# A gated long convolution beside a feed-forward layer on one core: a new opening, and a new written order for everything after it

## The chip, the cores and the metric

The kernel runs on one core of one Trainium2 chip. The metric is the device time of one execution in microseconds (us): 199.13 us before the change, the median of three runs that lie between 199.11 and 199.16 us. The core has five engines with a queue of instructions each: TensorE (PE in the profile: matrix multiplies and transposes, written to eight PSUM banks), VectorE (DVE), ScalarE (ACT: activations and copies), GpSimd (POOL, here mostly an issuer of DMAs) and SyncE (SP, which issues the other DMAs). An engine takes its instructions in the order in which they were written and stops at the first one whose inputs or buffers are not ready.

## The reference

All tensors are bf16 and the batch is 1: 2048 positions of 640 channels, and a hidden layer of 1728.

```python
x  = A_q
xn = layernorm(x)                                   # over the 640 channels
# branch A: short convolution, gate, long convolution by FFT, skip, gate
k_shift = sum_t k_pad[:, t:t+S] * shift_k[:, 3-t]   # 4 taps
kv = k_shift * A_v
y  = irfft(rfft(kv, 2S) * rfft(A_ssm_k, 2S))[:S] + kv * A_ssm_D
s  = xn * y
# branch B: feed-forward on the same normalised rows
g  = silu(gelu(xn @ w1 + b1) @ w2 + b2)
out = x + s * g
```

## The kernel before

**Tiling.** Position n of the sequence is row n // 16 of the 128 partitions and column n % 16. Sixteen consecutive columns make four chunks of four (`xn_tiles[c]`), and branch B goes chunk by chunk: `x_tr` (steps `tt`) transposes a normalised chunk into `xnT`, `ffn1` (`h`, 14 per chunk, five matmuls of 128x512 each; the last of a chunk has ten small ones) and its gelu on ACT (`he`) fill `hT`, `ffn2` (`g`, eight per chunk, 14 matmuls of 128x320 each) multiplies by w2, ACT takes the silu (`ge`), and DVE multiplies it into the normalised rows (`gm`).

**The long convolution** is a Fourier transform of 8192 points in two stages, written as matmuls with sine tables. The filter goes first: transposes (`kt`, cast out of PSUM by `kc`), first stage with the tables WA and WB (`kf`, out by `ke`), a store to DRAM that regroups the rows (`ks`), a load (`fl`), second stage (`ff`, out by `fe`), and a copy with swapped rows made by DMA (`mk`). The signal `kv` is built on DVE in 64 whole-row products and sums (`cv`), goes through the first stage (`uf`, out by `ue`), a store to DRAM (`us`) and a load (`ml`), and the second stage (`mu`). DVE multiplies it with the filter straight from PSUM, twice per tile (`mp`, `mq`: 96 products), PE transforms back (`ma`, `mb`, out by `me`), and after a last trip through DRAM (`ms` store, `yl` load) `y` does the last stage, `yt` multiplies with the rows of branch B and the result goes out (`yo`, `ys`; in the last chunk `ga`, `gs`).

**Small matmuls.** `ff`, `mu`, `ma` and `mb` work on 32 rows at a time. `blocks` (line 410) issues four matmuls of 32x32 weights for each of them; the table `TURNS` gives, for each of the 48 tiles of a stage, by how many places the output part is turned against the input part, so which four of the sixteen 32x32 parts of the array the four matmuls use.

**What sets the order.** No scheduler moves anything. `prologue()` writes the opening by hand: the constants, chunk 0's normalisation, transposes and the first six tiles of `ffn1`. Then a loop over the words of `PLAN` writes 1190 steps, one call each. A word is a step and its number, with `.a` or `.d` where either ACT or DVE can do it (casts out of PSUM, some normalisations). PSUM banks (`one`) and the SBUF slots of `area` (`pair`, `flat`) are handed out while this list is read, in its order, so a new order also changes which buffer a step takes and whom it has to wait for. `use_table` loads ACT's function tables where the order changes between gelu and the silu and sine set.

**The opening's end** (lines 823 to 843) goes: five tiles of `first_block(0, i)` on the first two columns, with a transpose of the packed small parameters `prm` behind the fourth; DVE's copy of the bias `b1_f` out of that transpose; the normalisation of columns 2 and 3; the copy `dD_sb`; the angles of the small 32x32 matrices (`small_bits`, `small_first`, `small_second`); the transposes `turn(2)`, `turn(3)`; the sixth `first_block`; `turned_out`, which copies those transposes to `xnT`, three fifths on DVE and two on ACT; and the six tiles of `first_block(1, i)` that read them.

## Time and profile before

| | us |
|---|---|
| median of 3 runs | 199.13 |
| the profiled execution | 199.48 |
| its span, first to last instruction | 197.7 |
| PE busy | 188.0 |
| DVE busy | 175.1 |
| ACT busy | 162.4 |
| POOL busy | 43.0 |

How to read it: busy time is the union of an engine's instructions; matmuls are pipelined and their ends are modelled, so two engines that are both near their span in busy time may differ a great deal in what they could still take. A row of the profile gives the line of the kernel, the engine, the operation, the tile written and read with its shape, a count, and the busy time with the mean duration of one. In the trace's rows by time, the second number is from the first start to the last end of a run of equal instructions. Consecutive instructions overlap at their ends, so that the distance between starts is shorter than a duration. A wait is put down to the instruction whose signal came last.

### The profile page before, as it was taken

Reading aid. Unit: us, or ns where it says so; the run is one execution under the profiler, and the core shown is the slowest. Engines: PE = TensorE matmul, PEld = TensorE weight load, DVE = VectorE, ACT = ScalarE, POOL = GpSimd, SP = SyncE. Lnnn points to the kernel's source line nnn. Section 1 sums busy time; section 2 is a strip of 40 time slices with the busy share of each in tenths; the row PEclk is TensorE's granted clock in tenths of the full one; section 3 lists DMA queues with packets and bytes.
Section 4 is the critical chain, followed back from the end, with each engine's and each line's share of the span. In section 5 each row is a group of like instructions: output and inputs, shape, how many; then the busy total and the mean of one; then the engine's idle time right before and its main releaser. Section 6 shows DMA issues by size and latency. Waiting matters only on the chain.

```text
span 197.7 us, 5098 instructions
## 1 busy us (share of the span) xinstructions
PE 188.0 (95%) x1913; PEld 110.7 (56%) x1925; DVE 175.1 (89%) x377; ACT 162.4 (82%) x322; POOL 43.0 (22%) x76
## 2 busy tenths in 40 slices
PE   7989989899999999998999999999999999999991
PEld 2566447786665455663565444365665544657770
DVE  7889998999999999989999999999999920489992
ACT  3458899999999999999998999999779758991030
POOL 8100200003455032255022000000466410002220
PEclk9999999999999999999999999999999999999999
DMA  6999999962878999798689899596869659994343
GB/s 202 375 385 348 355 411 412 395 243 103 328 302 339 297 318 368 275 360 323 252 277 332 260 356 317 196 297 239 254 243 339 237 169 327 395 396 184 148 175 138
DMA packets 27057, 57.69 MB, mean 292 GB/s; under 512 B 3032, under 2 KB 15513, under 8 KB 27032
## 3 DMA queue, kind: packets, MB, share of 16 engines
q1 hardware_dynamic: 22528, 39.65, 57.2%
q0 software_dynamic: 4320, 17.70, 24.1%
q8 instruction: 15, 0.25, 0.5%
q14 instruction: 10, 0.08, 0.2%
q10 hardware_dynamic: 184, 0.01, 0.1%
HBM read 33.76 MB, written 18.35 MB: 264 GB/s over the span
## 4 chain that ended last, share of the span: by engine, by line
PE 72%; ACT 17%; DVE 6%; issue 3%; POOL 0%; POOLq 0%; ACTq 0%; DVEq 0%
PE banks L493 23%; PE banks L467 21%; ACT area L147 8%; PE banks L414 7%; PE banks L533 5%; ACT hT L479 4%; PE banks L769 3%; PE banks L751 3%; PE banks L522 2%; PE banks L702 2%; ACT sl L499 2%; PE banks L451 2%; PE banks L703 2%; DVE area L573 2%; PE banks L463 1%
## 5 line engine op out<-in xcount | busy, mean ns | idle before, releaser
L147 ACT CAST area<-banks 128x426 bf16<-128x426 f32 (+2 forms) x175 | 80.7, 628 | 3.9 <-PE banks L414 3.4
L493 PE MATMUL banks<-w_sb,hT 128*128 128x320 bf16 x448 | 65.7, 299 | 0.5 <-ACT sl L499 0.4
L493 PEld LDWEIGHTS <-hT 128*128 128x128 bf16 x448 | 42.8, 98 | 19.5 <-issue 4.1
L467 PE MATMUL banks<-xnT,w_sb 128*128 128x512 bf16 x218 | 52.8, 379 | 0.7
L657 DVE TENSOR_TENSOR area<-banks,area 128x426 bf16<-128x426 f32 (+1 forms) x96 | 50.2, 594 | 0.2
L479 ACT ACTIVATE hT<-banks,b_f 128x512 bf16<-128x512 f32 x52 | 35.4, 719 | 5.6 <-PE banks L467 3.0
L467 PEld LDWEIGHTS <-w_sb 128*128 128x128 bf16 x230 | 21.5, 97 | 25.8 <-issue 3.7
L499 ACT ACTIVATE sl<-banks 128x320 bf16<-128x320 f32 x32 | 14.8, 489 | 14.5 <-PE banks L493 13.2
L577 DVE TENSOR_TENSOR area<-area 128x1280 bf16<-128x1280 bf16 x32 | 25.4, 818 | 0.3
L414 PE MATMUL banks<-area,mats 32*32 32x426 bf16 (+1 forms) x768 | 20.7, 345 | 0.5 <-DVE area L148 0.2
L711 DVE TENSOR_TENSOR area<-banks,xn 128x426 bf16<-128x426 f32 (+1 forms) x18 | 10.0, 595 | 12.3 <-ACT hT L479 10.2
L687 POOL DMA_DIRECT2D scrC<-area x16 | 11.7, 732 | 42.1 <-ACT area L147 40.0
L573 DVE TENSOR_TENSOR area<-area 128x1280 bf16<-128x1280 bf16 x24 | 19.1, 814 | 0.0
L533 PE MATMUL banks<-area,WA 128*128 128x212 bf16 (+1 forms) x64 | 15.6, 299 | 0.1
L548 POOL DMA_DIRECT2D scrK<-area x16 | 8.8, 554 | 30.2 <-DVE area L577 23.5
L533 PE MATMUL banks<-area,WB 128*128 128x214 bf16 (+1 forms) x64 | 15.3, 299 | 0.0
L414 PEld LDWEIGHTS <-mats 32*32 32x32 bf16 x768 | 8.1, 88 | 12.4 <-issue 10.1
L148 DVE CAST area<-banks 128x426 bf16<-128x426 f32 (+1 forms) x21 | 11.4, 594 | 1.7 <-PE banks L414 0.8
L559 POOL DMA_DIRECT2D scrU<-area x16 | 8.7, 546 | 14.7 <-ACT area L147 13.8
L430 POOL TENSOR_TENSOR rs<-ve,mhalf 128x4 f32<-128x4 f32 x3 | 4.1, 1351 | 31.1 <-DVE ve L426 31.1
L421 DVE BATCH_NORM_STATS2 st<-xn 128x6 f32<-128x320 bf16 x24 | 10.4, 473 | 0.0
L505 DVE TENSOR_TENSOR xn<-xn,sl 128x320 bf16<-128x320 bf16 x32 | 9.7, 314 | 0.7 <-ACT sl L499 0.7
(106 smaller groups left out, 198.3 us busy)
## 6 DMA issues: line engine op xcount, KB each, us to landing
scrK<-area POOLq DMA_DIRECT2D x16, 320.0 KB, 3.0
scrU<-area POOLq DMA_DIRECT2D x16, 320.0 KB, 4.1
area<-scrK SPq DMA_DIRECT2D x16, 320.0 KB, 6.5
area<-area SPq DMA_DIRECT2D x32, 160.0 KB, 4.2
area<-scrU SPq DMA_DIRECT2D x16, 320.0 KB, 4.2
scrC<-area POOLq DMA_DIRECT2D x16, 320.0 KB, 4.2
area<-scrC SPq DMA_DIRECT2D x16, 320.0 KB, 6.6
area<-in_A_k_dram SPq DMA_DIRECT2D x4, 640.0 KB, 10.0
```

The lines of the kernel that those rows point to most:

```text
L147: return nc.scalar.copy(out=out_ap, in_=in_ap)
L148: return nc.vector.tensor_copy(out=out_ap, in_=in_ap)
L414: nc.tensor.matmul(out=out[b, :], lhsT=mats[a, m, a], rhs=rhs[a, :], start=start, stop=stop)
L467: nc.tensor.matmul(out=ps, lhsT=w1_sb[:, t, ft * P:(ft + 1) * P], rhs=xnT[:, t, :], start=(t == 0), stop=(t == DT - 1))
L479: nc.scalar.activation(out=hT[:, ft, :], in_=one(("h", i)), func=ACT.Gelu_apprx_tanh, bias=b1_f[:, ft:ft + 1], scale=1.0)
L493: nc.tensor.matmul(out=ps[:, 0:HALF], lhsT=hT[0:M, ft, q * P:(q + 1) * P], rhs=w2_sb[0:M, ft, hs], start=(ft == 0), stop=(ft == FT - 1))
L499: nc.scalar.activation(out=sl[:], in_=one(("g", i))[:, 0:HALF], func=ACT.Silu)
L533: nc.tensor.matmul(out=ps[:, dst], lhsT=(WA, WB)[r][:, n2, :], rhs=rows[:, n2 % 2, src], start=True, stop=True)
L573: nc.vector.tensor_tensor(out=uc, in0=uc, in1=tmp, op=ALU.add)
L577: nc.vector.tensor_tensor(out=tmp if s else uc, in0=kh[:, r0:r0 + KC, :], in1=w_exp[:, j:j + 1, :].to_broadcast([P, KC, D]), op=ALU.mult)
L657: nc.vector.tensor_tensor(out=flat(("p", i))[:, x * w:x * w + w], in0=one(("mu", i))[:, 0:w], in1=flat(key)[:, cols(j)], op=ALU.mult)
L687: nc.gpsimd.dma_start(out=pair_view(scrC)[g2], in_=pair(("c", g2)))
```

## The change

Three things are changed. In the opening, the transpose of `prm` goes behind `turn(3)` and into the free half of bank 7, the copies of `b1_f` and `dD_sb` go behind `turned_out`, the sixth tile of `first_block` behind them, and the angles of `small_second` (with one that was in `small_first`) go last. `PLAN` is a new list of the same 1190 steps: every step but the opening stands at a new place, and some have another engine. `TURNS` is a new table.

```diff
-TURNS = "231221331312001123202202330111320201303303312100"
+TURNS = "222121231121032230103232000033311030021012210212"
 PLAN = """
-em6 he0 he1 s w X1 em7 em5 he2 K1 em4 ls6 ls7 ls4 ls5 K0 h11 he5 ee5.a ee4.a h8 h6 he4 ee7.a he3 he8 B1 h13 B2 B0 cv16
+ir em5 em4 w s X1 he1 he0 ls7 K1 ls6 ls4 ls5 cv16 lv1 lr1 he3 he2 he4 K0 cv8 cv9 h11 ee4.a em7 ee7.a ee5.a h13 he13 h9
...
@@ small_first, small_second
-        stt(sm["ph"][:, 0, :], n_out, n_in[:, 0:1], c_out, ALU.mult, ALU.add)
...
+        stt(ph[:, 0, :], n_out, n_in[:, 0:1], c_out, ALU.mult, ALU.add)
         stt(ph[:, 2, :], n_out, n_in[:, 0:1], c_out, ALU.mult, ALU.subtract)
@@ prologue
-        pt = banks[:, 5, :].bitcast(BF16)
+        pt = banks[:, 7, :].bitcast(BF16)[:, 4 * P:]
...
         for i in range(NFIRST - 1):
             first_block(0, i)
-            if i == 3:
-                nc.tensor.transpose(out=pt[:, 0:FT + DT], in_=prm[:, :], identity=ident[0:FT + DT, 0:FT + DT])
-        nc.vector.tensor_copy(out=b1_f[:], in_=pt[:, 0:FT])
         sq(2)
         rc(2)
         norm_dve(2)
         norm_dve(3)
-        nc.vector.tensor_copy(out=dD_sb[:], in_=pt[:, FT:FT + DT])
         small_bits(96)
         small_first()
-        small_second()
         nc.scalar.activation(out=sd[:, 0:1], in_=eps[:], func=ACT.Gelu_apprx_tanh)
         turn(2)
         turn(3)
-        first_block(0, NFIRST - 1)
+        nc.tensor.transpose(out=pt[:, 0:FT + DT], in_=prm[:, :], identity=ident[0:FT + DT, 0:FT + DT])
         turned_out("d", 0, 1)
         turned_out("a", 1, 1)
+        nc.vector.tensor_copy(out=b1_f[:], in_=pt[:, 0:FT])
+        nc.vector.tensor_copy(out=dD_sb[:], in_=pt[:, FT:FT + DT])
+        first_block(0, NFIRST - 1)
+        small_second()
         for i in range(NFIRST):
             first_block(1, i)
```

Counted in the two lists, the choice of an engine changes as follows (steps on ACT and on DVE, before and now): `fe` 38 and 10, now 35 and 13; `ue` 41 and 7, now 43 and 5; `kc` 5 and 11, now 4 and 12; `ln` 6 and 6, now 5 and 7; `me` 46 and 2, now 45 and 3; `te` 6 and 9, now 7 and 8; `ke`, `ee`, `gm` and `yo` as before. Function tables are loaded at as many places as before.

Three places of the new order in rows. The changed file is two lines shorter, so its line numbers are one or two less.

DVE at the end of the opening, before (`xn` the rows of chunk 0, `b_f` the bias, `xnT` the transposed rows, `area` here the small angles):

```order
L827 CAST b_f<-banks 128x14
L740 RECIPROCAL rstd<-sd 128x2
L743 TENSOR_SCALAR xn<-xn,mv,rstd 128x640 x2
L832 COPY dD_sb<-banks 128x5
L350 TENSOR_SCALAR area<-area 128x1
L352 CAST area<-area 128x1
L362 TENSOR_SCALAR area<-area 128x1
L363 TENSOR_SCALAR area<-area 128x1
L356 SCALAR_TENSOR_TENSOR area<-area 128x128 x2
L371 TENSOR_SCALAR area<-area 128x128
L148 COPY xnT<-banks 128x3x256
```

The same place on DVE now:

```order
L739 RECIPROCAL rstd<-sd 128x2
L742 TENSOR_SCALAR xn<-xn,mv,rstd 128x640 x2
L349 TENSOR_SCALAR area<-area 128x1
L351 CAST area<-area 128x1
L361 TENSOR_SCALAR area<-area 128x1
L362 TENSOR_SCALAR area<-area 128x1
L147 COPY xnT<-banks 128x3x256
L836 CAST b_f<-banks 128x14
L837 COPY dD_sb<-banks 128x5
L355 SCALAR_TENSOR_TENSOR area<-area 128x128 x2
L370 TENSOR_SCALAR area<-area 128x128
```

The bias copy no longer stands ahead of the normalisation, and three products of 128x128 and one copy no longer stand ahead of the copy to `xnT`.

DVE at the normalisation of chunk 1, some 20 rows later, before (`xn` chunk 1, `area` the signal's products, line 577, and sums, line 573):

```order
L577 TENSOR_TENSOR area<-area 128x1280 x3
L434 SCALAR_TENSOR_TENSOR nb_362<-mv_300,rs_360 128x4
L573 TENSOR_TENSOR area<-area 128x1280
L577 TENSOR_TENSOR area<-area 128x1280
L573 TENSOR_TENSOR area<-area 128x1280
L444 TENSOR_SCALAR xn<-xn,mv_300,rs_360 128x640 x2
L577 TENSOR_TENSOR area<-area 128x1280
```

And now:

```order
L576 TENSOR_TENSOR area<-area 128x1280 x3
L433 SCALAR_TENSOR_TENSOR nb_388<-mv_301,rs_318 128x4
L572 TENSOR_TENSOR area<-area 128x1280
L576 TENSOR_TENSOR area<-area 128x1280 x3
L443 TENSOR_SCALAR xn<-xn,mv_301,rs_318 128x640 x3
L572 TENSOR_TENSOR area<-area 128x1280 x2
```

One more product of the signal stands ahead of the normalisation, and DVE normalises three columns of the chunk there in place of two.

POOL before, from the opening's last fill to the stores of the inverse stage (`rs` the chunks' inverse deviations, `kcol`, `kn`, `kj` the index tables of the last stage, step `ir`):

```order
L790 MEMSET area 1x1920
L430 TENSOR_TENSOR rs_360<-ve_354,mhalf 128x4
L548 DMA scrK<-area 128x1280 x16
L559 DMA scrU<-area 128x1280 x2
L430 TENSOR_TENSOR rs_961<-ve_910,mhalf 128x4
L559 DMA scrU<-area 128x1280 x14
L430 TENSOR_TENSOR rs_1432<-ve_1430,mhalf 128x4
L595 IOTA kcol 128x1
L597 IOTA kn 128x128
L598 TENSOR_SCALAR kn<-kn,kcol 128x128
L597 IOTA kj 128x16
L598 TENSOR_SCALAR kj<-kj,kcol 128x16
```

And now:

```order
L789 MEMSET area 1x1920
L594 IOTA kcol 128x1
L596 IOTA kn 128x128
L597 TENSOR_SCALAR kn<-kn,kcol 128x128
L596 IOTA kj 128x16
L597 TENSOR_SCALAR kj<-kj,kcol 128x16
L429 TENSOR_TENSOR rs_318<-ve_316,mhalf 128x4
L547 DMA scrK<-area 128x1280 x16
```

The index tables moved from behind the last `us` store into the opening.

## The prediction

> **What bounds the kernel now.** The page's first lines and its chain of work name TensorE:

> ```profile
> PE 188.0 (95%) x1913; PEld 110.7 (56%) x1925; DVE 175.1 (89%) x377; ACT 162.4 (82%) x322; POOL 43.0 (22%) x76
> ...
> PE 72%; ACT 17%; DVE 6%; issue 3%; POOL 0%; POOLq 0%; ACTq 0%; DVEq 0%
> ```

> Three engines are that close together, so an average says little. The view of busy time by stretches, cut at 154.97 us, where DVE ends its last product, and at 169.62, where its next long run starts, tells them apart:

> ```profile
> 36.00:97.00 61.00, 59.47 (x495) 36.56 (x496) 59.34 (x113) 60.87 (x138) 19.06 (x33) 1.00 0.82 302
> 97.00:154.97 57.97, 57.10 (x909) 30.51 (x912) 57.70 (x124) 52.77 (x109) 12.46 (x20) 1.00 0.84 279
> 154.97:169.62 14.65, 14.54 (x109) 7.20 (x111) 3.96 (x9) 11.22 (x19) 1.63 (x3) 1.00 0.74 255
> ```

> The columns after the length are PE, PE's weight loads, DVE, ACT and POOL. ACT is full to 97 us, DVE to 155, and after that only PE is. So there are two stages: up to the last product DVE's list must be worked off, and then PE still has fixed work to do. What DVE waited for between 14 and 155 us, from the view of its waits in that window, is all of this:

> ```profile
> DVE mats L394 <- ACT area L390: 0.6, 1, 0.6
> DVE area L148 <- ACT area L147: 0.5, 1, 0.5
> DVE area L148 <- PE banks L533: 0.4, 2, 0.2
> DVE area L148 <- PE banks L414: 0.3, 1, 0.3
> ```

> That is 1.8 us in 141. Each of the five also loses some 0.08 us of the overlap between neighbours (a cast lasts 0.59 to 0.60 us, the next starts after 0.51), so 2.2 us in all. PE, whose busy time is modelled, has more room. From its rows by time:

> ```profile
> 143.03 0.58 PE L414 MATMUL banks<-area,mats 32*32 32x428 bf16 x32
> 143.55 2.08 PE L493 MATMUL banks<-w_sb,hT 128*128 128x320 bf16 x14
> ...
> 148.08 0.90 PE L414 MATMUL banks<-area,mats 32*32 32x426 bf16 x48
> ...
> 157.44 4.48 PE L467 MATMUL banks<-xnT,w_sb 128*128 128x512 bf16 x19
> ...
> 169.00 0.34 PE L702 MATMUL banks<-area,WA 128*128 128x426 bf16 x1
> 169.18 0.34 PE L703 MATMUL banks<-area,WB 128*128 128x426 bf16 x1
> ...
> 187.67 5.88 PE L493 MATMUL banks<-w_sb,hT 128*128 128x320 bf16 x42
> ```

> A `g` takes 5.88 us less a last overlap of 0.17 over three, 1.90; an `h` five times (4.48 - 0.38) / 19, 1.08. I add up the starts alone: 32 `g` are 61 us, 46 `h` and four short ones 52, 24 `y` of two such steps of 0.18 us 9, the 96 first-stage tiles of one step each 17, and 26 groups of 32x32 blocks at 0.6 to 0.9 us 18; with some 8 for the transposes that is about 165 us, where PE ran from the opening's end at 17.5 to 193.4 us, 175.9. Some 9 us or more of that stretch were waits, spread too thin to see. I therefore take DVE as the bound up to the last product. [...]

> **The change, step by step.** *Opening.* Both engines' rows by time, where PE waits for the second copy to `xnT`:

> ```profile
> 12.73 0.71 PE L769 MATMUL banks<-xnT,w_sb 128*128 128x256 bf16 x5
> 14.18 1.03 PE L769 MATMUL banks<-xnT,w_sb 128*128 128x256 bf16 x8 [0.74 <-DVE xnT L148]
> ...
> 11.30 0.17 DVE L827 CAST b_f<-banks 128x14 f32<-128x14 bf16 x1 [0.75 <-PE banks L826]
> ...
> 12.74 0.60 DVE L356 SCALAR_TENSOR_TENSOR area<-area 128x128 f32<-128x128 f32 x2
> 13.38 0.29 DVE L371 TENSOR_SCALAR area<-area 128x128 f32<-128x128 f32 x1
> 13.58 0.55 DVE L148 COPY xnT<-banks 128x768 bf16<-128x768 bf16 x1
> 14.05 0.22 DVE L377 TENSOR_SCALAR area<-area 128x128 f32<-128x128 f32 x1
> ```

> DVE stood 0.75 us for the parameter transpose, and the two products and the sum (0.84 us from start to start) stood ahead of the copy. Without both, the normalisation comes 0.7 us sooner, the transposes start right behind PE's fifth tile, and the copy as soon as eight of the ten are done, at about 12.3 us, and PE goes on at 12.9 in place of 14.18: 1.27 us. DVE has the small copies and the angles behind it (0.47 + 0.16 + 0.84 us) and starts the next row at 13.8 in place of 14.05: **-0.3 us**. PE's gain is spent soon after:

> ```profile
> 27.83 0.90 PE L451 MATMUL banks<-ident,xn 128*128 128x128 bf16 x13 [0.52 <-ACT xn L442]
> ...
> 28.37 1.28 ACT L315 ACT_TABLE_LOAD   x1
> ...
> 31.67 0.60 ACT L390 ACTIVATE area<-area,sin_bias 128x384 f32<-128x384 int32 x1
> ```

> Transposes of chunk 1 need all of its rows, of which DVE normalised the first two at 26.23 us (row below). Now it begins 0.3 us earlier with one product more ahead of it (2.29 less 0.82 over two, 0.74) and does three of 0.36: they are done at 27.7, so PE transposes at 27.8 as before. ACT is early instead. Its gelus start some 0.7 us sooner behind PE's earlier tiles and it has one normalisation fewer, 0.8 us, so the table load of the second row moves to about 26.9 us and the sine of the third, with a cast of `xnT` now ahead of it (0.5), to about 30.7. DVE comes to `mats` at 32 us or later: the first of the four waits goes.

> *DVE's list.* From start to start, by rows of equal neighbours:

> ```profile
> 21.54 2.29 DVE L577 TENSOR_TENSOR area<-area 128x1280 bf16<-128x1280 bf16 x3
> ...
> 26.23 0.80 DVE L444 TENSOR_SCALAR xn<-xn,mv,rs 128x640 bf16<-128x640 bf16 x2
> ...
> 37.32 1.68 DVE L148 COPY area<-banks 128x640 bf16<-128x640 bf16 x4
> ...
> 88.21 5.72 DVE L148 CAST area<-banks 128x426 bf16<-128x426 f32 x11 [0.55 <-ACT area L147]
> ...
> 97.97 1.43 DVE L148 COPY xnT<-banks 128x512 bf16<-128x512 bf16 x4
> ...
> 96.42 4.70 ACT L147 CAST area<-banks 128x426 bf16<-128x426 f32 x11
> ...
> 151.82 3.15 DVE L657 TENSOR_TENSOR area<-banks,area 128x428 bf16<-128x428 f32 x6
> ```

> Up to the last product DVE gets one cast more (5.72 - 0.60 over ten, 0.51), one `kc` more (0.40) and one normalisation more (0.36), and one `te` less (0.34): **+0.9 us**; by the durations instead of the starts it would be 1.1. ACT loses some 2.3 us of work (a cast is 0.41 there), which counts for nothing where DVE is the later one.

> *DVE's waits.* 2.2 us before. The sine's goes (0.7). The others were casts that came too soon after ACT or PE: with ACT a further 1.3 us ahead at the first `kc`, each cast on DVE now stands about 4 us behind the end of the work that it empties, by the sums of starts up to it, where those four stood 2 to 3 behind. Against that, a copy of `xnT` at 33 us stands just behind its transposes (0.3), and a new list has surprises. I keep 0.8 us, between 0 and the 2.2 of before: **-1.4 us**.

> *After the last product.* Both lists end with the same kinds of work on PE, behind one last group of blocks. Behind it stand now eight `g` in place of nine, twelve full `h` and a short one in place of ten and a short one, and all 24 `y` as before: two `h` more, 2.16, and one `g` less, 1.90, make +0.25. The group itself stands 0.1 us nearer to the product, as `g23` covers it. **+0.15 us**, from -0.2 to +0.8. What could open a gap is the trip through DRAM before `y`:

> ```profile
> 155.67 1.11 DVE L148 CAST area<-banks 128x428 bf16<-128x428 f32 x2 [0.47 <-PE banks L414]
> ...
> 161.25 2.23 SPq L694 DMA_DIRECT2D area<-scrC  x5
> ...
> DMA to landing us min/median/max: 3.2/6.6/8.4
> ```

> The last casts ended at 156.8, the first load went out at 161.25, and the first `y` stands at 169.0 in the rows above without a wait. The first of these loads lands soonest, in some 3.2 to 4 us, so there were about 4 us of cover. Now the last cast comes about 2 us later against the row of `h`, and that row is 1.1 us longer: it covers the trip still. If it did not, that would cost what is missing, up to 1 us.

> *Groups and TURNS.* Two groups of blocks in the rows above, eight blocks in 0.58 us and twelve in 0.90, show what a repeat of the same array parts costs (about 0.2 us a round). The new list has 27 groups in place of 26 (0.7) and some three more rounds (0.6): 1.3 us more of PE. It lies in PE's 9 us of room, so nothing; with PE as the bound it would be all of it. SP's and POOL's queues carry the same transfers in a new order; of those, one is priced as a rival.

> Sum: -0.3 + 0.9 - 1.4 + 0.15 = **-0.65 us**. The profiled execution took 199.48 us (span 197.7 and 1.8 around it), 0.35 above the median; so 198.8 for such a run and **198.5 us** as a median.

> **The rivals.** *PE is the bound*: for it, the chain's 72%; against it, the 9 us. Opening -1.27 and groups +1.3: 199.1 us.

> *The signal's trip through DRAM becomes late* (the slower side). The last `us` stores, the first `ml` loads and the first product:

> ```profile
> 91.40 1.61 POOL L559 DMA_DIRECT2D scrU<-area  x3 [0.48 <-ACT area L147]
> ...
> 96.66 2.42 SPq L639 DMA_DIRECT2D area<-scrU  x3
> ...
> 102.13 1.11 DVE L657 TENSOR_TENSOR area<-banks,area 128x426 bf16<-128x426 f32 x2
> ```

> From the last store's end to the load 3.7 us, from the load to the product 5.5. DVE's own rows between its last signal cast and the first product are 11.1 us before and 10.9 now, so there is no more cover than there was, and a filter load that went out at 111.7 us before now stands ahead of those loads in SP's queue. It decides when the first product comes over 12 us after that cast. With 1.6 us of it uncovered: 198.5 + 1.6 = 200.1 us.

> *No wait is left on DVE*: 0.8 us less, 197.7 us.

> *GpSimd's index tables disturb the opening.* They ran beside products, and now beside DVE's first normalisations:

> ```profile
> L598 POOL TENSOR_SCALAR kn<-kn,kcol 128x128 int16<-128x128 int16 x1 | 0.6, 612 | 0.1
> ```

> If DVE stood still for it, 0.6 us: 199.1. [...]

> **How the numbers follow.** Forecast 0.48, its own range 197.9 to 199.0; PE the bound 0.14; the late trip 0.21; no wait 0.12; GpSimd 0.05. A measurement of this kernel tells about 0.2%, 0.4 us, from no change. Faster by more: the forecast but for its upper edge (0.44) and no wait, 0.56. Within: that edge (0.04), PE and GpSimd, 0.23. Slower: 0.21. The range, 197.3 to 200.4 us, takes in all but the ends of the outer two: it holds the ends of DVE's waits (0 and 2.2 us) and of the last stage.

> **What would show it.** PE's wait of 0.74 us before the second half of chunk 0 gone, and the next row at 12.9; no wait of `mats` for the sine; `g1` still at 28.5 us; DVE without gaps until its last product, which ends near 153.8; 37 to 39 us from there to PE's end. The forecast is wrong if DVE shows waits of over 2 us before its last product, most likely at the first ones, or if PE shows a gap among the last `h` and `y`.

## The result, and the profile after

| | kernel before | changed kernel |
|---|---|---|
| median, us | 199.16 (20 runs, 199.11 to 199.40) | 200.63 (20 runs, 199.60 to 203.23) |
| changed to before, 95% interval | | 1.0069 (1.0048 to 1.0091) |
| the profiled execution, us | 199.48 | 202.18 |
| its span, us | 197.7 | 200.4 |

The change costs 0.7% where the prediction had a gain of 0.3%. The median hides two groups, which the mean granted TensorE clock of each run tells apart: ten runs with a clock of 0.996 or more lie between 199.60 and 200.03 us (median 199.7), ten with 0.991 or less between 201.2 and 203.2 (median 201.4). The profiled execution, with 0.988, is of the second group and among its longest. So there are two questions: what is worth 1.7 us in half of the runs, and why the other half is 0.5 us above the kernel before.

From the page of the changed kernel, the busy shares, the granted clock in 40 slices of 5 us, and the chain of work that ended last, by engine and by line:

```profile
PE 186.8 (93%) x1913; PEld 112.2 (56%) x1925; DVE 176.3 (88%) x380; ACT 161.4 (81%) x319; POOL 45.1 (22%) x76
...
PEclk9999988999999999999999999999999999999998
...
PE 67%; DMA 12%; ACT 7%; DVE 7%; POOL 2%; issue 2%; SPq 1%; ACTq 0%; POOLq 0%
PE banks L492 28%; PE banks L466 20%; PE banks L413 7%; DMA area<-in_A_k_dram 6%; PE banks L532 6%; ACT area L146 4%; DMA w_sb<-in_B_w_dram 3%; DVE area L147 3%; DMA area<-in_A_ssm_k_dram 3%; PE banks L701 2%; PE banks L702 2%; POOL rs L429 2%; ACT sl L498 2%; PE banks L450 2%; DVE area L576 1%
```

Two things are new: loads in the chain, and two slices, from 25 to 35 us, in which TensorE's clock was not granted in full (the low clock in the last slice lies behind the last computation). Busy time by stretches cuts each trace where DVE starts its list (14.05 us before, 13.73 now), where its last product ends, and where its last instruction ends. The kernel before, with the columns length, PE, weight loads, DVE, ACT, POOL:

```profile
14.05:154.97 140.92, 137.71 (x1560) 80.64 (x1569) 138.06 (x281) 133.23 (x272) 32.99 (x54) 1.00 0.86 305
154.97:194.74 39.77, 38.34 (x281) 23.57 (x282) 26.07 (x58) 22.53 (x39) 4.91 (x9) 1.00 0.69 251
194.74:197.70 2.96, 0.00 (x0) 0.00 (x0) 0.00 (x1) 0.00 (x0) 0.00 (x0) 1.00 0.24 81
```

And the changed kernel:

```profile
13.73:157.08 143.35, 136.93 (x1555) 81.66 (x1563) 138.52 (x283) 131.57 (x268) 32.15 (x47) 0.99 0.86 303
157.08:196.76 39.68, 38.28 (x278) 23.30 (x278) 26.66 (x59) 23.23 (x40) 6.25 (x11) 1.00 0.68 243
196.76:200.39 3.63, 0.00 (x0) 0.00 (x0) 0.00 (x0) 0.00 (x0) 0.00 (x0) 0.83 0.20 69
```

DVE's busy time, the fourth value, hardly moves (138.06 to 138.52), but its list takes 2.4 us longer: these are waits. The long stretch behind the last product is the same. A stretch in which no engine computes grew from 2.96 to 3.63 us; the prediction had no term for it. DVE's waits from 13 to 157 us, the four largest:

```profile
DVE area L576 <- DMA area<-in_A_k_dram: 1.2, 1, 1.2
DVE xnT L147 <- PE banks L450: 1.2, 1, 1.2
DVE nb L433 <- POOL rs L429: 0.9, 1, 0.9
DVE area L656 <- PE banks L413: 0.3, 2, 0.2
```

None of them was there before. The rows of DVE and PE by time around the first two:

```profile
22.52 2.29 DVE L576 TENSOR_TENSOR area<-area 128x1280 bf16<-128x1280 bf16 x3 [1.20 <-DMA area<-in_A_k_dram]
...
25.73 2.29 DVE L576 TENSOR_TENSOR area<-area 128x1280 bf16<-128x1280 bf16 x3
...
27.94 1.15 DVE L443 TENSOR_SCALAR xn<-xn,mv,rs 128x640 bf16<-128x640 bf16 x3
...
29.15 1.46 PE L450 MATMUL banks<-ident,xn 128*128 128x128 bf16 x12 [3.76 <-DVE xn L443]
...
30.40 2.82 PE L492 MATMUL banks<-w_sb,hT 128*128 128x320 bf16 x14
```

DVE waits 1.2 us for a load of `k`, so the normalisations of chunk 1 come late, and PE, which reached them early thanks to the new opening, stands for 3.76 us. Then its own work is slow: twelve transposes and a `g` take 1.46 and 2.82 us, where they take 0.84 and 2.07 in e7 below, at the full clock. In stretches of 2 us (the third value from the end is the granted clock):

```profile
24.00:26.00 2.00, 1.39 (x7) 0.43 (x5) 1.89 (x5) 1.08 (x2) 0.00 (x0) 1.00 1.04 406
26.00:28.00 2.00, 0.00 (x0) 0.00 (x0) 2.00 (x4) 1.98 (x3) 0.00 (x0) 1.00 1.03 397
28.00:30.00 2.00, 0.85 (x9) 0.85 (x10) 2.00 (x6) 1.99 (x3) 0.00 (x0) 0.63 1.04 416
30.00:32.00 2.00, 2.00 (x13) 1.34 (x12) 1.97 (x3) 2.00 (x4) 0.00 (x0) 0.52 1.00 402
32.00:34.00 2.00, 2.00 (x19) 1.50 (x18) 2.00 (x5) 1.28 (x1) 0.00 (x0) 1.00 1.03 397
```

With 0.37 and 0.48 of two microseconds missing, that is 3.4 us at half speed; the trace's own records of the clock have it at half from 28.51 to 31.92 us. Spread over a run of 198 us it makes a mean clock of 0.991; seven of the slower group's ten runs show 0.990 or 0.991. PE's delay comes back to DVE as the second wait, for transposes.

### The profile page after: what moved, and what is told of

The parts are those of the page before. It is cut to its first block, busy times and chain, and to the rows that moved or that the text cites. A ratio compares the mean times of both kernels' runs of the same rounds, so it can differ in the third digit from the quotient of the medians.

```text
span 200.4 us, 5106 instructions
## 1 busy us (share of the span) xinstructions
PE 186.8 (93%) x1913; PEld 112.2 (56%) x1925; DVE 176.3 (88%) x380; ACT 161.4 (81%) x319; POOL 45.1 (22%) x76
## 4 chain that ended last, share of the span: by engine, by line
PE 67%; DMA 12%; ACT 7%; DVE 7%; POOL 2%; issue 2%; SPq 1%; ACTq 0%; POOLq 0%
PE banks L492 28%; PE banks L466 20%; PE banks L413 7%; DMA area<-in_A_k_dram 6%; PE banks L532 6%; ACT area L146 4%; DMA w_sb<-in_B_w_dram 3%; DVE area L147 3%; DMA area<-in_A_ssm_k_dram 3%; PE banks L701 2%; PE banks L702 2%; POOL rs L429 2%; ACT sl L498 2%; PE banks L450 2%; DVE area L576 1%
## 5 line engine op out<-in xcount | busy, mean ns | idle before, releaser
L146 ACT CAST area<-banks 128x426 bf16<-128x426 f32 (+2 forms) x173 | 77.0, 550 | 4.8 <-PE banks L413 3.9
L492 PEld LDWEIGHTS <-hT 128*128 128x128 bf16 x448 | 43.4, 98 | 19.9 <-issue 3.3
L478 ACT ACTIVATE hT<-banks,b_f 128x512 bf16<-128x512 f32 x52 | 33.8, 698 | 3.3 <-PE banks L466 1.9
L498 ACT ACTIVATE sl<-banks 128x320 bf16<-128x320 f32 x32 | 13.6, 443 | 16.7 <-PE banks L492 11.4
L532 PE MATMUL banks<-area,WA 128*128 128x428 bf16 (+1 forms) x64 | 15.9, 299 | 0.1
L413 PEld LDWEIGHTS <-mats 32*32 32x32 bf16 x768 | 9.0, 88 | 11.8 <-issue 8.8
L147 DVE CAST area<-banks 128x426 bf16<-128x426 f32 (+1 forms) x23 | 13.1, 593 | 0.3 <-PE banks L413 0.3
L429 POOL TENSOR_TENSOR rs<-ve,mhalf 128x4 f32<-128x4 f32 x3 | 6.1, 2021 | 21.3 <-DVE ve L425 21.3
```

What stands on the lines that cost most here:

```text
L146: return nc.scalar.copy(out=out_ap, in_=in_ap)
L147: return nc.vector.tensor_copy(out=out_ap, in_=in_ap)
L413: nc.tensor.matmul(out=out[b, :], lhsT=mats[a, m, a], rhs=rhs[a, :], start=start, stop=stop)
L478: nc.scalar.activation(out=hT[:, ft, :], in_=one(("h", i)), func=ACT.Gelu_apprx_tanh, bias=b1_f[:, ft:ft + 1], scale=1.0)
L492: nc.tensor.matmul(out=ps[:, 0:HALF], lhsT=hT[0:M, ft, q * P:(q + 1) * P], rhs=w2_sb[0:M, ft, hs], start=(ft == 0), stop=(ft == FT - 1))
L498: nc.scalar.activation(out=sl[:], in_=one(("g", i))[:, 0:HALF], func=ACT.Silu)
```

## The experiments

Thirteen kernels were run, one of them twice (e9 and e9b). Medians, with the ratio to the kernel before on the same chip:

| kernel | us, median (lowest to highest), runs | ratio, 95% interval |
|---|---|---|
| e1 opening alone | 198.34 (198.25 to 198.45), 6 | 0.9950 (0.9938 to 0.9962) |
| e2 normalisations first | 200.21 (199.85 to 200.44), 6 | 1.0041 (1.0028 to 1.0054) |
| e4 old TURNS | 203.11 (202.05 to 203.83), 6 | 1.0185 (1.0155 to 1.0215) |
| e5 old opening | 199.90 (199.69 to 200.14), 10 | 1.0025 (1.0016 to 1.0035) |
| e6 filled gap | 200.12 (199.85 to 201.09), 8 | 1.0045 (1.0030 to 1.0061) |
| e7 last store by SyncE | 200.54 (198.86 to 200.85), 12 | 1.0042 (1.0020 to 1.0063) |
| e8 power early | 199.50 (198.65 to 200.68), 12 | 1.0014 (0.9990 to 1.0037) |
| e9 three edits | 197.90 (197.87 to 197.91), 5 | 0.9925 (0.9913 to 0.9937) |
| e9b the same again | 197.98 (197.94 to 198.08), 5 | 0.9934 (0.9920 to 0.9947) |
| e11 fewer rounds | 197.85 (197.78 to 197.95), 5 | 0.9928 (0.9916 to 0.9941) |

Four more were run once, each for one duration in its trace: e10 199.29 us, e12 199.21, e13 204.41 and e14 199.79.

**e1, the opening alone.** The kernel before with the new lines of `prologue`, `small_first` and `small_second`; `PLAN` and `TURNS` stay.

> The kernel before with the new opening alone (old order, old TURNS). Theory A (the loss is made at chunk 1 by the new order: three more products, one of them waiting 1.2 us for a load, stand ahead of its last normalisations, PE stands still for 3.8 us and its clock then runs at half speed for 3.4 us): the opening by itself keeps the 0.3 us that DVE starts earlier, 198.7 to 199.1 us, every run at a clock of 0.996 or more. Theory B (the new opening itself costs the time, by a PE that runs ahead and then waits): 199.6 us or more, with some runs over 201.

Measured: 198.34 us, 0.9 less than before and a little better than expected; all six runs within 0.2 us. Its waits on DVE from 13 to 157 us are those of before without the one of `mats` for the sine (0.6) and one of 0.2:

```profile
DVE area L148 <- PE banks L414: 0.8, 2, 0.5
DVE area L148 <- ACT area L147: 0.5, 1, 0.5
DVE area L148 <- PE banks L533: 0.2, 1, 0.2
```

So the wait of the sine, which the prediction counted under the new order, belongs to the opening, and the new order and table together cost 1.4 us in the faster group and 3.1 in the slower one.

**e2, e6, e5: the gap at chunk 1.** Three ways to take PE's long stand away: e2 moves three steps in `PLAN`, e6 lets PE work in it, e5 puts the old opening ahead of the new order, so that PE comes later.

```diff
 e2, PLAN:
-... C4 cv10 cv11 cv0 cv1 he8 ws0 ln5.d ln7.d ln4.d tt5 ...
+... C4 ln5.d ln7.d ln4.d cv10 cv11 cv0 cv1 he8 ws0 tt5 ...
 e6, x_tr:
         tp = one_bf(("tt", i))
+        if i == 5:
+            for _ in range(10):
+                nc.tensor.matmul(out=one(("tt", i)).rearrange("p (a b) -> p a b", a=4), lhsT=ident[:],
+                                 rhs=ident[:, None, :].to_broadcast([P, 4, P]), start=True, stop=True)
```

> The changed kernel with the three last normalisations of chunk 1 (ln5 ln7 ln4) directly behind the first (ln6), ahead of cv10 cv11 cv0 cv1, as DVE's row order alone. Theory A: DVE ends them about 3 us sooner (three products and a sum, 3.1 us, stand behind them now), PE waits some 0.7 us in place of 3.8, the clock stays at 1.0 in that stretch, no run lies over 201 us, and DVE's wait of 1.2 us for the transposes goes: 198.6 to 199.6 us. Theory C (the loss is PE's own, from the groups of small blocks in the new order): 199.6 us or more still, in one cluster. Theory D (the low clock comes from elsewhere): two clusters as before, 199.6 to 200.0 and 201.2 to 202.

> The changed kernel with ten matmuls of 128x512 that nobody reads (2.2 us) in PE's wait at 25.4 us, written to the bank of the transposes that wait. They change no other engine's rows. Theory A: the wait for the normalisations stays (PE goes on at 29.1 us where the load is late), but TensorE is busy in it, so the half clock goes: no run over 200.3 us, all runs in the cluster of 199.6 to 200.0. Theory D (the low clock has nothing to do with the gap): two clusters as before.

> The changed order and TURNS with the old opening. The opening alone was worth 0.9 us under the old order. Theory A (PE's gap before chunk 1 decides whether its clock halves): PE comes to the gap 1.3 us later, so the gap is some 1.3 us long in place of 2.6 (3.8 with a late load) and no run has the half clock; DVE starts 0.3 us later: 199.9 to 200.4 us, one cluster. Theory B (opening and gap are independent): 0.9 us later than the changed kernel in both of its clusters, 200.6 and 202.3.

Measured: in none of the 24 runs of the three is the clock below 0.993 or the time above 201.1 us; the slower group is gone. Two forecasts were missed all the same: e2 is slower than theory A allowed, and e6 has three runs at 200.4 to 201.1 us with a clock of 0.995 or more, whose cause no trace shows. PE's rows at chunk 1 in e6 (the ten matmuls, then the transposes, still waited for):

```profile
25.23 2.32 PE L451 MATMUL banks<-ident 128*128 128x512 bf16 x10
27.86 0.84 PE L454 MATMUL banks<-ident,xn 128*128 128x128 bf16 x12 [0.31 <-DVE xn L443]
28.54 2.07 PE L496 MATMUL banks<-w_sb,hT 128*128 128x320 bf16 x14
```

The normalisations come no sooner there, and work that nobody reads takes the slower group away: it is the clock, not the lateness, that costs 1.7 us. In e5's trace the stand is 1.16 us long, in the trace of e7 below, which is the changed kernel at this place, 2.46:

```profile
27.85 0.84 PE L450 MATMUL banks<-ident,xn 128*128 128x128 bf16 x12 [2.46 <-DVE xn L443]
```

So 2.5 us of it is the usual length, and the clock falls in some runs (9 of 12 of e7, 10 of 20 of the changed kernel, by their mean clock) and not in others; the 3.76 us of the profiled run is the rarer case with the late load on top. The trace of e13 below, which is the changed kernel at this place too, caught the usual case: no load is late, the stand is 2.47 us, and the clock halves. Its PE rows:

```profile
27.87 1.38 PE L450 MATMUL banks<-ident,xn 128*128 128x128 bf16 x12 [2.47 <-DVE xn L443]
29.04 3.23 PE L492 MATMUL banks<-w_sb,hT 128*128 128x320 bf16 x14
```

The traces bear on why only some runs are hit. Counted from a trace's first record of the clock, every change of it lies at a whole multiple of 3.413 us: in e13 the first record is at 4.10 us, the changes at 27.99, 31.40, 86.02 and 89.43; in the changed kernel 4.61, and 28.51, 31.92 and 199.17; before 7.36, and 198.50. Cut into windows on that grid, the stretch around the stand is this in e13, in e8 and in e7:

```profile
24.58:27.99 3.41, 0.94 (x7) 0.32 (x5) 3.41 (x7) 3.30 (x6) 0.00 (x0) 1.00 1.03 410
27.99:31.40 3.41, 3.41 (x21) 2.41 (x20) 3.38 (x5) 3.41 (x4) 0.00 (x0) 0.50 1.02 409
...
24.19:27.60 3.41, 1.42 (x7) 0.45 (x5) 3.30 (x7) 3.31 (x4) 0.00 (x0) 1.00 1.02 406
...
23.21:26.62 3.41, 2.18 (x11) 0.78 (x8) 3.30 (x6) 3.24 (x5) 0.00 (x0) 1.00 1.05 404
26.62:30.03 3.41, 2.18 (x24) 1.76 (x25) 3.38 (x7) 3.40 (x5) 0.00 (x0) 1.00 1.02 408
```

In e13 the whole stand, 2.47 us, lies in one window and the clock halves in the next (as in the changed kernel's trace, where PE stands 3.12 us of the window from 25.10 to 28.51); in e8 and e7 an edge cuts it, into at most 1.99 and 1.23 us, and the clock stays full. e13 has a second such stretch: PE stood 1.95 us in one window, for a product that the moved cast held up, and ran at half clock from 86.02 to 89.43 us. Behind the last matmuls, 2.14 us (e4) and 2.17 us (e1) of one window were followed by half clock in the next, too. In these traces half clock thus came behind stands of 1.95, 2.14, 2.17, 2.47 and 3.12 us of one window, and not behind 1.99 or 1.23. My estimate from that, with 2 us as the dividing line: 1.9 of the 3.4 us of possible positions give a stand of 2.46 us that much of one window, 55%; 24 of the 44 runs of the changed kernel, e7 and e8 show a mean clock of 0.991 or less.

No other profile of this order shows DVE waiting for that load; what delayed it there was not tried. Theory B of e5 falls, since its 0.9 us did not come back: with the old opening in front the new order takes 199.9 us, 0.2 more than the faster group.

But e2, in which PE goes from its last `h` to the transposes without a stand, isn't faster than the faster group: 200.2 us in one cluster is what theory C, PE's own work as the limit, had forecast. DVE's row of its first product points elsewhere, and e11 below speaks against C:

```profile
102.65 1.62 DVE L656 TENSOR_TENSOR area<-banks,area 128x426 bf16<-128x426 f32 x3 [0.71 <-PE banks L413]
```

There it waits, as PE did 0.5 us for a load of the signal (`scrU`): the late trip, the prediction's rival, in a small form. It starts at 102.04 in e7.

**e7, the end.** The view of the closing rows (line 890 before, 888 now; columns: count, shortest, median and longest in ns, first and last start). Before:

```profile
L890 POOLq DRAIN  x3: 40/93/5052, 190.9 to 197.4; - x3
L890 SPq DRAIN  x3: 7/7/7, 196.9 to 197.2; - x3
```

And the changed kernel:

```profile
L888 POOLq DRAIN  x3: 40/93/5502, 194.1 to 200.1; - x3
L888 SPq DRAIN  x3: 7/7/7, 198.9 to 199.9; - x3
```

From its last output store on GpSimd drains for 5.1 us before and 5.5 us now, which is the longest of its three drains, taken to be the one that began first. Before, that was over at 196.0, 0.9 us ahead of SyncE's own; now at 199.6, 0.7 us behind it. So GpSimd sets the end.

```diff
-        nc.gpsimd.dma_start(out=out_v[:, 2 * i:2 * i + 2, :], in_=pair(("o", i)))
+        (nc.sync if i == 4 else nc.gpsimd).dma_start(out=out_v[:, 2 * i:2 * i + 2, :], in_=pair(("o", i)))
```

> The changed kernel with the last of GpSimd's six output stores issued by SyncE instead. Theory E (the end is set by GpSimd, whose closing drain lasts 5.0 to 5.8 us from its last store and ended 0.8 us behind everything else in the changed kernel, but 1 us ahead of the end before): the end follows SyncE's last landing by 1.3 us as before, so 0.7 to 0.8 us less in either cluster, about 199.0 and 200.6. Rival (the drain is only recorded long and something else ends the execution): no change.

Measured: 198.86 to 198.98 us in three runs, 200.5 to 200.9 in nine, 0.8 us below the changed kernel's two groups. Its profiled run is of the faster group:

```profile
13.73:154.50 140.77, 135.65 (x1555) 80.73 (x1563) 138.32 (x283) 131.62 (x268) 32.66 (x47) 1.00 0.88 309
154.50:194.17 39.67, 38.27 (x278) 23.34 (x278) 26.65 (x59) 23.24 (x40) 5.70 (x10) 1.00 0.67 243
194.17:197.08 2.91, 0.00 (x0) 0.00 (x0) 0.00 (x1) 0.00 (x0) 0.00 (x0) 1.00 0.25 86
```

The first two lengths are also what the undisturbed changed order takes (e6: 140.80 and 39.67); the third is 2.91 in place of e6's 3.87.

**e8, the power.** `ln_root` computes a chunk's inverse deviations on GpSimd. For chunk 2, in the changed kernel, with DVE's rows beside it:

```profile
81.17 0.81 DVE L576 TENSOR_TENSOR area<-area 128x1280 bf16<-128x1280 bf16 x1
81.91 1.55 DVE L572 TENSOR_TENSOR area<-area 128x1280 bf16<-128x1280 bf16 x2
83.38 0.81 DVE L565 TENSOR_TENSOR area<-area 128x1280 bf16<-128x1280 bf16 x1
84.12 0.32 DVE L504 TENSOR_TENSOR xn<-xn,sl 128x320 bf16<-128x320 bf16 x1
85.37 0.16 DVE L433 SCALAR_TENSOR_TENSOR nb<-mv,rs 128x4 f32<-128x4 f32 x1 [0.94 <-POOL rs L429]
```

```profile
81.35 3.98 POOL L429 TENSOR_TENSOR rs<-ve,mhalf 128x4 f32<-128x4 f32 x1 [0.26 <-DVE ve L425]
```

It lasts 3.98 us, and DVE, which reads the result, stands for 0.94. e8 moves two words:

```diff
-... ue40.a cv31 cv33 cv60 ... us11 us3 cv34 ue22.d cv61 lv2 lr2 cv35 ...
+... ue40.a lv2 lr2 cv31 cv33 cv60 ... us11 us3 cv34 ue22.d cv61 cv35 ...
```

> The changed kernel with the step of GpSimd's power for chunk 2 (and the small DVE step ahead of it) moved ahead of the two us stores, some 5 us earlier, where GpSimd has issued nothing for ten us. It takes 4.0 us right behind a store's issue, 1.0 to 1.5 us elsewhere, and DVE waits 0.9 us for it. Theory F (GpSimd computes late behind a DMA issue): 1.0 to 1.6 us, no wait on DVE, and 0.5 to 0.9 us less time in either cluster. Rival G (DVE's long products between SBUF tiles shut GpSimd out): it stays at 3 to 4 us, as such products run there too.

Measured: the power takes 1.54 us, the wait is gone, and the runs lie at 198.65 to 199.88 us (seven, median 198.96) and 200.3 to 200.7 (five): 0.7 and 0.9 us less than the changed kernel. The size is as expected; the reason given for it isn't, as the next four show.

**e10, e12, e13, e14: why 4 us.** e10 and e12 move the power in the kernel before; e13 and e14 change what stands beside it in the changed kernel.

```diff
 e10:
-... ue16.a lr2 cv57 lb2 h20 ... fl7 us9 ue39.a ... ff38 ln10.d ...
+... ue16.a cv57 h20 ... fl7 us9 lr2 ue39.a ... ff38 lb2 ln10.d ...
 e12:
-... uf24 cv26 ... ue17.a cv44 lv2 cv54 ... ue16.a lr2 cv57 ...
+... uf24 lv2 lr2 cv26 ... ue17.a cv44 cv54 ... ue16.a cv57 ...
 e13:
-... ff10 cv36 cv63 gm6.d lb2 fe7.d uf21 ...
+... ff10 fe7.d cv36 cv63 gm6.d lb2 uf21 ...
 e14:
-... us11 us3 cv34 ue22.d cv61 lv2 lr2 cv35 ...
+... us11 cv34 ue22.d cv61 lv2 lr2 us3 cv35 ...
```

> The kernel before with GpSimd's power for chunk 2 moved from ten us behind its last store issue to right behind the store of us9, and DVE's step that reads it moved on to the normalisations, some 7 us later, so that nobody has to wait. The opposite of the last edit on the power. Theory F (GpSimd computes late behind a DMA issue): the power lasts 3.5 to 4.5 us in place of 1.54, whatever DVE does. Rival G (DVE's products shut it out): it depends on DVE's rows and stays near 1.5 where casts out of PSUM stand between the products.

> The kernel before with DVE's small step and GpSimd's power for chunk 2 moved up by two sums, so that three sums of the signal (two whole SBUF operands each, 2.3 us from first start to last end) follow the small step without a pause, with a product by the tap row behind them. A store's issue was ruled out by e10. Theory G (a run of such DVE instructions keeps GpSimd's power waiting until the last of them has ended, and only products by a tap row or casts let it through; in the changed kernel it ended 0.9 us behind the last of five such rows): the power lasts some 3 us here. Rival H (it waits for the one DVE instruction that runs when it comes, as in the rows of 1.5 us, and the 4.0 us have another cause): 1.5 us.

> The changed kernel with one cast out of PSUM (fe7) moved up between the sums and products that follow the small step on DVE, while GpSimd's power of 4.0 us runs. PE's tile for it comes some 1.5 us later, so DVE also pauses there. Theory K (behind a store's issue, GpSimd's power gets on only when DVE's run of instructions with two SBUF operands has a pause): it ends some 0.9 us into that pause, after 2.0 to 2.5 us. Rival L (a fixed delay of that place, whatever DVE does): 4.0 us still.

> The changed kernel with the store just ahead of the power (us3) moved behind it; the one before that (us11, 2 us earlier) stays. DVE's rows are the same. Theory K: without a store right ahead the power takes 1.5 us beside the same run of sums and products, and DVE does not wait. Rival M (that run of DVE alone, at this place, keeps it out): 4.0 us still.

Measured, in GpSimd's rows of e12 and of e14 (e10: 1.04 us at 77.35, right behind two stores; e13: 2.28 us at 80.40):

```profile
68.44 1.54 POOL L430 TENSOR_TENSOR rs<-ve,mhalf 128x4 f32<-128x4 f32 x1 [5.60 <-DVE ve L426]
```

```profile
78.82 3.98 POOL L429 TENSOR_TENSOR rs<-ve,mhalf 128x4 f32<-128x4 f32 x1 [1.67 <-DVE ve L425]
```

A store ahead of it does nothing: with it alone 1.04 us (e10), without it 3.98 still (e14). In e13, where DVE pauses behind its second row, the power ends 0.9 us behind that row's end; in the changed kernel and in e14 it ends 0.9 us behind the fifth row, the last ahead of DVE's pause. So at this place its end goes with DVE's rows and not with a store, rival M. But in e12 it also came into a run of such rows and ended 0.9 us behind the first of them. No run shows what makes the power end behind the first row at some places and only behind the last at this one. That stays open. The 204.41 us of e13 come with two stretches of 3.41 us at half clock and a wait of 1.67 us on DVE for the cast that was moved.

**e4 and e11: PE's room.** Two other tables `TURNS` change only how often the groups of small blocks repeat the same array parts: by an estimate of 0.19 us a repeat (the prediction's two groups of blocks, 0.58 and 0.90 us, gave about 0.2), 5.0 us more on PE than the new table in the changed kernel, and 1.6 us less in e9. (In the traces the busy time of the small blocks grew by 3.6 us from e7 to e4, and fell by 0.5 us from e9b to e11.)

```diff
 e4:
-TURNS = "222121231121032230103232000033311030021012210212"
+TURNS = "231221331312001123202202330111320201303303312100"
 e11, on e9:
-TURNS = "222121231121032230103232000033311030021012210212"
+TURNS = "210332032210212033211030310112133321300120100022"
```

> The changed kernel with the old TURNS. By the rounds that the groups of small blocks now take (0.19 us for each repeat of the same array parts) PE has 5.0 us more work than with the new table. Theory A with the prediction's 9 us of room on PE: most of it is hidden, under 1 us slower than the changed kernel's clusters. Theory C (PE is the bound up to the last product): 4 to 5 us slower, 204 to 205 us in the undisturbed runs.

> The changed kernel with the three edits (e9) and another TURNS, chosen so that the groups of small blocks repeat the same array parts less often: by 0.19 us a repeat, 1.6 us less on PE in the whole kernel. Theory A (PE has room for that): within 0.2 us of e9. Theory C (PE is the bound up to the last product): 1 to 1.6 us faster, 196.3 to 196.9. By what e4 showed (2.3 of 5.0 us came through) about 0.5 to 0.7 us faster, 197.2 to 197.4.

Measured: e4 took 202.05 to 202.49 us (median 202.3) in its three runs with a clock of 0.993 or more, 2.6 more than the faster group, so about half of the 5.0 came through, between what the two theories had forecast. Its DVE waits are now for the small blocks:

```profile
DVE area L656 <- PE banks L413: 1.2, 4, 0.4
DVE nb L433 <- POOL rs L429: 0.9, 1, 0.9
DVE area L147 <- PE banks L413: 0.7, 2, 0.5
```

e11 took 197.85 us, 0.13 less than e9b on the same chip, of 1.6. With the new table and the three edits, fewer rounds on PE gain next to nothing; by the estimate, some 2.4 us more of them and they begin to cost.

**e9, together.** The edits of e2, e7 and e8; e9b is the same text again.

> The changed kernel with the normalisations of chunk 1 first, the power early and the last store on SyncE. If the three causes add up: e2's 200.2 less 0.75 (end) less 0.5 to 0.9 (power) is 198.5 to 199.0 us in one cluster, below the kernel before by 0.2 to 0.7 and still above the old order with the new opening (198.3). If DVE's list is not the bound up to the last product, the power's share is missing: 199.4.

> e9 once more, for the comparison with e11 on the same chip: 197.9 us within 0.1 on a chip where the kernel before takes 199.2, all runs in one cluster.

Measured: 197.90 and 197.98 us, all ten runs within 0.2 us, 0.6 us better than forecast; 2.3 us below e2, where the two further edits were good for 1.5 to 1.7. The rest is about the size of e2's wait at the first product, which is under 0.2 us in e9. Why the load came late in e2 is not shown: e7 has the signal's stores behind the power in GpSimd's queue too, its last of them and its loads go out within 0.1 us of e2's (stores at 91.40 and 91.46 us, loads from 96.33 and 96.39), and its first product waits 0.16. The stretch up to the last product, now with 1.5 us of waits in all:

```profile
13.78:153.56 139.78, 135.93 (x1555) 81.19 (x1563) 138.25 (x283) 131.42 (x268) 30.43 (x47) 1.00 0.88 311
```

This is 0.7% below the kernel before and 0.4 us below the opening alone, so the new order is worth something once these three places are put right.

## Why the prediction was wrong

Its sum was -0.3 + 0.9 - 1.4 + 0.15. In the stretches of the traces, undisturbed (with a full clock and no late load: e7, and e6 for the end) and as profiled:

| term | predicted | undisturbed | profiled run |
|---|---|---|---|
| DVE's start | -0.3 | -0.3 | -0.3 |
| DVE's list (busy time) | +0.9 | +0.3 | +0.5 |
| DVE's waits (length less busy) | -1.4 | -0.4 | +2.0 |
| last product to DVE's end | +0.15 | -0.1 | -0.1 |
| DVE's end to the end | none | +0.9 | +0.7 |
| sum, us | -0.65 | +0.4 | +2.7 |

*Opening: held.* PE began the second half of chunk 0 without its wait of 0.74, at about 12.6 us in place of 14.18, and DVE started 0.3 us sooner. By itself it is worth 0.9 us, as e1 shows, more than this term, since the sine's 0.6 us belongs to it too.

*"PE's gain is spent soon after": the step that failed for the slower group.* The place and the time were right, 27.85 us in e7 against 27.8. But the gain was spent as idle time of TensorE, 2.5 us where there had been half a microsecond, and I priced idle time at nothing. In half of the runs the clock then halves for 3.4 us, which delays transposes on which DVE soon waits (1.4 us in e13). e6 takes it away with work that nobody reads, e5 by giving the gain up, e2 by moving the normalisations. The order put one product more ahead of them, and I had quoted the rows that show it.

*DVE's waits: the step that failed for the other group.* The four waits of before went as I said, but "a new list has surprises" was priced at 0.8 us; the undisturbed length less busy time is 2.45 us in e7 (2.86 before, of which the prediction had counted 2.2), of which 0.94 is the wait for the power. A power that lasted at most 1.54 us in the trace of before took 4.0. With it gone (e9), that difference is 1.53: the -1.4 was there to be had.

*The list* was sized by single instructions and came out at a third, which no run explains; *after the last product* the covers held, as said, within 0.25.

*The end: a term that was missing.* I ended the sum at PE's and DVE's last rows and let SyncE's last store follow as before. GpSimd's last store stood 3.8 us ahead of DVE's end before, 2.6 now, and behind it the drain of 5 us.

*Groups and TURNS* cost next to nothing, as predicted (e11 got back 0.13 of 1.6 us), but not for the reason given: PE had no 9 us that could be used anywhere. e4 shows about 2.4, by the same estimate of 0.19 us a repeat.

Of the rivals, the late trip came true once, in e2, at 0.6 us; GpSimd's index tables disturbed nothing (DVE's first two normalisations start at 6.60 us and take 0.81, 6.61 and 0.80 before, though `kn` runs from 6.28 to 6.89 us beside them, so DVE did not stand still for it); PE as the bound is refuted by e11, and approached in e4; "no wait left" did not come, with 2.45 us left in e7. None of them was the case that happened.

## What to carry to other kernels

When a wait on TensorE moves, look at how long the engine then stands still, not only at who is late: here a stand of 2.5 us that no sum noticed went with 1.7 us more in half of the changed kernel's runs, where the opening that made it was worth 0.9 us, and filler work (e6), or work moved into it, is the test. Follow every engine to its last instruction, GpSimd's drain behind its last store among them (5.05 to 5.73 us here), and give the final stores to a queue that ends sooner (0.8 us less in e7). For short GpSimd steps look at what DVE runs beside them, since a step of 1.03 us at one place took 3.98 us at another.

## What was not expected of the hardware

GpSimd's power of 128x4 took 1.03 to 1.05 us where it started beside a cast (changed kernel at 102.30 us, e10 at 77.35), beside a product out of PSUM (before at 102.35) or while DVE waited (changed kernel at 21.40), 1.48 to 1.54 us when it met a running DVE product or sum of two SBUF operands (before at 21.79 and 70.20 us, e8, e12), and 3.98 us in one place (changed kernel at 81.35 us, e14; 2.28 us there in e13), with no change of its own.

GpSimd's closing drain took 5.05 us before, 5.50 us in the changed kernel and 5.73 us in e6, from the issue of its last store.
